# Attention and gated FFN on one core: four query/key buffers, one bias transfer for two heads, three value transfers issued first

## The chip, the cores and the metric

The kernel runs on one core of one Trainium2 chip. The metric is the device time of one execution in microseconds; the time before is the median of three executions.

## The reference

Four batches, eight heads, 576 positions, head size 64; then a gated FFN with 512 inputs and 1024 hidden columns. All inputs are float32.

```python
scores = scale * np.matmul(q, k.transpose(0, 1, 3, 2))
x = (psi_rel / psi_i)[..., None]          # log distances, from positions alone
h = np.maximum(x @ w1 + b1, 0.0)
bias = h @ w2                             # one value per (i, j, head)
scores = scores + bias.transpose(2, 0, 1)[None, :, :, :]
attn = softmax(scores)
y = np.matmul(attn, v)
# FFN on y: relu(y @ w_in), a 3-tap convolution along the sequence,
# h * sigmoid(conv), @ w_out
```

## The kernel before

**Bias first.** The bias depends on the positions and the head only. A first stage (some 66 us) computes it for all eight heads, 36 blocks of 16 rows, and writes it to a DRAM scratch tensor, bias_d (L292). Attention reads it back from there as tiles of 128 rows.

**Pairs and units.** Attention then goes over 16 pairs n = 0 to 15. A pair is two heads p (0 to 3) of one batch b, with b running fastest, so the heads change, and with them the bias tiles, between pairs 3 and 4, 7 and 8, 11 and 12. A pair has five units t = 0 to 4, of 128 rows each: unit 0 holds the 64 remaining rows of both heads, units 1 to 4 hold 128 rows of each head. The list of units is `flat`; the loop over it (L635 on) is written out by hand as a software pipeline. Step (n, t) issues the scores (L349, TensorE) and the `reduce` (L360, VectorE: scores plus bias, row minimum) of the unit two places on, the exponentials (L374, ScalarE) of the next unit, the transposes (L420) of its own unit, and some parts of the product with the values (L457). So the bias tile t of the next heads is first read at step (n, t − 2) of the last pair before them or of their own first pair; tile 4 is the last one that is read, at step (4, 2), (8, 2) or (12, 2).

**Order of issue.** Every engine works through its own instructions in order. Nearly all transfers are issued by SyncE (SP) on one queue, in the order in which the program lists them; an SP instruction that waits holds up all that stand behind it.

**What SP issues in a pair.** In step (n, 2): queries and keys of pair n + 2 (`load`, four transfers, L150 and L151, 950 KB), which go into the buffer of pair n, one of two in pool `q_p`, and so wait until TensorE has done the last scores of pair n, issued in the same step. In every second step a slice of the FFN's weights (`load_w`, L118, 256 KB), read by VectorE and ScalarE four to five steps later. In the steps where the loop issues the last reduce that reads a bias tile of the old heads: the same tile of the next heads (`load_bias`, tile 0 in L178, tiles 1 to 4 in L176, one transfer for each head, 128 rows of 2304 bytes). In (n, 2), last: the values of pair n + 1 (`load_v`, L165 to L168, four transfers, 288 KB), into the buffer of pair n − 1, after the last product that reads it (in the same step). In (n, 3) and (n, 4): the softmax sums of pair n − 1 out to DRAM (L483 to L485) and back, spread over the partitions (L490), for GpSimd (L497).

**Pool `raw_p`.** It has two buffers with the tag "raw". One is used as a staging tile in the bias stage, and both from pair 14 on for the FFN's split inputs (`x_parts`). Between these uses they stand empty.

Of the kernel before, what the change touches and what calls it, by code (L numbers as in the profile page):

```python
# [9 lines left out]
F32 = mybir.dt.float32  # L10
# [9 lines left out]
def attention_ffn_kernel(  # L20
# [11 lines left out]
    nc = tc.nc  # L32
    B, S, DM = out.shape
    NP = qk.shape[1]
    D = qk.shape[2]
# [3 lines left out]
    P = 128  # L39
    TL = S % P  # L40
# [6 lines left out]
    BW = S + 64  # L47
# [6 lines left out]
    KO = 2 * QW  # L54

    def halves(ap):
        return ap.rearrange("p (a b) -> p a b", a=2)

    def pool(stack, name, bufs, **kw):
        return stack.enter_context(tc.tile_pool(name=name, bufs=bufs, reuse_waits="tile", **kw))  # L60
# [7 lines left out]
    raw_p = pool(ctx, "raw", 2)  # L68
# [11 lines left out]
    bias_rows = bias_d[64:64 + S * (H * BW - 1)].rearrange("(i c) -> i c", c=H * BW - 1)  # L80
# [3 lines left out]
    NSEQ = len(seq)  # L84
# [49 lines left out]
    with tc.manual_schedule():  # L134
        att = ExitStack()
        q_p = pool(att, "q", 2)
# [4 lines left out]
        vts, qks, sms, biast = {}, {}, {}, {}  # L141


        def load(n):
            p, b = seq[n]
            qks[n] = t = q_p.tile([P, KO + S], F32, name="qk")
            keys = qk[b, p, :, KO:].rearrange("d (h a s) -> d a h s", h=2, a=2)
            for a in range(2):
                rows = slice(D * a, D * a + D)
                nc.sync.dma_start(t[rows, 0:KO], qk[b, p, :, 0:KO])  # L150
                nc.sync.dma_start(halves(t[rows, KO:]), keys[:, a])  # L151
# [10 lines left out]
        def load_v(n):  # L162
            p, b = seq[n]
            vts[n] = vt = v_t[n % 2]
            nc.sync.dma_start(vt[0:TL, 0:9], v[b, p, 0:TL, 0:9])  # L165
            nc.sync.dma_start(vt[TL:P, 0:4], v[b, p, TL:P, 0:4])
            nc.sync.dma_start(vt[TL:P, 5:9], v[b, p, TL:P, 5:9])
            nc.sync.dma_start(vt[TL:P, 9], v[b, p, TL:P, 4])  # L168

        def load_bias(p, t):  # L170
            bt = bias_p.tile([P, 2, S], F32, name="bt") if t else bias0_p.tile([P, 1, S], F32, name="bt0")
            for h in range(2):
                c = (2 * p + h) * BW
                if t:
                    i0 = TL + (t - 1) * P
                    nc.sync.dma_start(bt[:, h], bias_rows[i0:i0 + P, c:c + S])  # L176
                else:
                    nc.sync.dma_start(bt[TL * h:TL * h + TL, 0, :], bias_rows[0:TL, c:c + S])  # L178
            biast[p, t] = bt

# [151 lines left out]
        def scores(n, t, h):  # L332
            p, b = seq[n]
            qt = qks[n]
            if h == 0:
                if n not in sms:
                    sms[n] = sm_p.tile([P, 9], F32, name="sm")
                nms[n, t] = sm_p.tile([P, 2], F32, name="nm")
                new_sp(n, t)
            ps = psS.tile([P, 2, 512], F32, name="s")  # L340


            ops = [(h, h * QW + P * t, slice(0, P))] if t else [
                (hh, hh * (QW + TL), slice(TL * hh, TL * hh + TL)) for hh in range(2)
            ]
            for hh, qo, po in ops:
                for a in range(2):
                    rows = slice(D * a, D * a + D)
                    nc.tensor.matmul(  # L349
                        ps[po, a, 0:HS],  # L350
                        qt[rows, qo:qo + po.stop - po.start],
                        qt[rows, KO + hh * HS:KO + hh * HS + HS],
                        start=True,
                        stop=True,
                    )
            return ps

        def reduce(ps, n, t, h):
            bt = biast[seq[n][0], t]
            nc.vector.tensor_tensor_reduce(  # L360
                out=halves(spt[n, t][0][:, h]),
                in0=ps[:, :, 0:HS],
                in1=halves(bt[:, h]),
                op0=ALU.add,
                op1=ALU.min,
                scale=-scale,
                scalar=3.0e38,
                accum_out=nms[n, t][:, h:h + 1],
            )
# [34 lines left out]
        def side_transposes(side, n, t, sums):  # L404

            spf = spt[n, t][0]
            for a, ra in enumerate(halves_):
                tr = nc.tensor.transpose(side[:, a, HS:HS + TL].bitcast(F32R), spf[ra, 8 * P:9 * P], identr[ra, ra])  # L408
                after_exp(tr, n, t)
            if sums is not None:  # L410
                for a, ra in enumerate(halves_):
                    nc.tensor.transpose(side[:, a, HS + TL:HS + P], rr_t[sums % 2][ra], ident[ra, ra])
# [154 lines left out]
        def heads(t):  # L567
            return (0, 1) if t else (0,)
# [66 lines left out]
        for u, (n, t) in enumerate(flat):  # L635
            p, b = seq[n]
            ui = units.index(t)
            sums = n - 1 if ui == 2 and n else None
            side = None
            if u + 2 < NU:  # L640
                for h in heads(flat[u + 2][1]):
                    if side is not None:
                        reduce(side, *flat[u + 2], 0)
                    side = scores(*flat[u + 2], h)
            if t:
                if side is None:
                    side = psS.tile([P, 2, 512], F32, name="s")
                side_transposes(side, n, t, sums)
            if u + 2 < NU:
                reduce(side, *flat[u + 2], h)  # L650
            if u + 1 < NU:
                for h in heads(flat[u + 1][1]):
                    expo(*flat[u + 1], h)
                turned_sp(*flat[u + 1])
            transposes(n, t, side, sums)
            next(job_steps, None)

            parts = len(fill) if u < 5 else pv_share[ui]
            while fill and parts > 0:
                fill.popleft()()  # L660
                parts -= 1
            next(job_steps, None)
            del spt[n, t]
            if u + 2 >= NU:
                f = u + 2 - NU
                hs_ff[0, f] = ffn_in(0, f)
            if u == 1 or n and ui == 2 and n + 2 < NSEQ:
                load(2 if u == 1 else n + 2)
            if u in conv_weights:
                conv_weights[u]()  # L670

            for at, do in ((u - 7, "load"), (u - 11, "split")):
                job = at // 2
                if at % 2 == 0 or not 0 <= job < 4 * KC + 2 * FE:
                    continue
                if job < 4 * KC:
                    src, dst = w_in[job // 4 * P:job // 4 * P + P], wi[job // 4]
                else:
                    src, dst = w_out[(job - 4 * KC) // 2 * P:(job - 4 * KC) // 2 * P + P], wo[(job - 4 * KC) // 2]
                cs = slice(job % 4 * 256, job % 4 * 256 + 256) if job < 4 * KC else slice(job % 2 * 256, job % 2 * 256 + 256)  # L680
                if do == "load":
                    raw_w[job] = (e_p if job % 3 else woe_p).tile([P, 256, 2], I32, name="raw_w", tag="h")
                    load_w(raw_w[job], src[:, cs])
                else:
                    job_steps = split_w_steps(e_p, dst[:, :, cs], raw_w.pop(job), ("cv", "cv"))
            if u + 2 < NU:
                n2, t2 = flat[u + 2]
                p2, b2 = seq[n2]
                if b2 == B - 1 and p2 + 1 < NP:
                    load_bias(p2 + 1, t2)  # L690
            if ui == (0 if n > 1 else 1) and n > 0:
                invert(n - 1)
            if ui == (2 if n > 1 else 3) and 1 <= n and n + 1 < NSEQ:
                load_v(n + 1)
            if ui == 3 and n > 0:
                store_sums(n - 1)
            if ui == 4 and n > 0:
                spread_sums(n - 1)
            if ends_group(n, t):
                fill.extend(pv_parts(n, t > 2))  # L700

            if ui == 2 and n > 1:
                apply_norm(n - 2)
            if n == NSEQ - 2 and ui > 1:
                x_parts(0, ui - 2)
            if n == NSEQ - 1 and ui == 0:
                x_parts(0, 3)
            if n == NSEQ - 1 and ui in (1, 2):
                load_wo(FE - 1 + ui)
# [91 lines left out]
        for i, (b, f) in enumerate(steps):  # L801
            if b == 0 and f in (2, 4):
                c = FE - 1 + f // 2
# [10 lines left out]
            for c in range(KC):  # L814
# [5 lines left out]
                lambda f, gi, t=t: gs[b, f][:, gi, t * P:(t + 1) * P] for t in range(NT)  # L820
# [98 lines left out]
```

## Time and profile before

| | |
|---|---|
| median of three executions | 500.37 us (498.35 to 500.55) |
| the profiled execution | 503.5 us |
| its span, first to last instruction | 501.7 us |
| TensorE busy in the span | 481.3 us |
| granted TensorE clock, mean | 0.997 |
| attention, pair after pair | about 84 to 300 us |

The views give times in microseconds from the start of the span. PE is TensorE's matmuls, PEld its weight loads, DVE VectorE, ACT ScalarE, POOL GpSimd, SPq SyncE's queue of transfers. A row of a timeline gives start, length, engine, line, operation, what is written from what, and how often; in square brackets the engine's idle time before it and what ended that. A row of windows gives one stretch: its length, the busy time of each engine with its number of instructions, the granted clock (1.00 is 2.4 GHz, 0.50 is 1.2 GHz), the mean busy share of the 16 DMA engines, and what they moved in GB/s.

### The profile page before, as it was taken

What the parts mean: (1) busy time and instruction counts of PE and PEld (TensorE: products, weight loads), DVE (VectorE), ACT (ScalarE), POOL (GpSimd) and SP (SyncE); (2) the same over time, 40 slices, a digit from 0 to 9 for tenths busy, and PEclk for the clock granted to TensorE, in tenths of its full rate; (3) what the DMA queues carried; (4) which work ended last, traced back from release to release, by engine and by line L of the source; (5) the groups of instructions that cost most, each with busy time, mean ns of one, the idle gap of its engine ahead of it and who ended that gap; (6) DMA issues with size and microseconds to landing.
All of it is one profiled execution on the core that took longest, in us unless ns stands there. A gap on an engine that the chain in (4) does not pass through costs nothing.

```text
span 501.7 us, 11124 instructions
## 1 busy us (share of the span) xinstructions
PE 481.3 (96%) x4202; PEld 354.0 (71%) x4202; DVE 383.3 (76%) x875; ACT 311.8 (62%) x747; POOL 103.6 (21%) x121
## 2 busy tenths in 40 slices
PE   5988889999999999999899999899999999999997
PEld 3333346666666666666466679779998899899986
DVE  6999957788888988998588918993896189829920
ACT  5988777878888889888488738541541145215510
POOL 1000000103232323223235513650052003400000
PEclk9999999999999999999899999999999999999999
DMA  5689556488778977879672300002000200020011
GB/s 135 256 265 338 204 176 149 108 238 207 183 176 202 260 173 169 181 190 273 173 185 59 109 25 26 0 2 84 1 1 0 106 0 2 1 84 1 0 43 64
DMA packets 32793, 60.83 MB, mean 121 GB/s; under 512 B 5580, under 2 KB 12260, under 8 KB 32740
## 3 DMA queue, kind: packets, MB, share of 16 engines
q1 hardware_dynamic: 32356, 59.78, 42.6%
q8 instruction: 33, 0.54, 0.5%
q10 hardware_dynamic: 384, 0.35, 0.2%
q14 instruction: 20, 0.16, 0.1%
HBM read 44.12 MB, written 15.98 MB: 120 GB/s over the span
## 4 chain that ended last, share of the span: by engine, by line
PE 82%; DVE 6%; DMA 5%; ACT 4%; issue 2%; SPq 0%; DVEq 0%; ACTq 0%
PE s L518 17%; PE o L457 16%; PE tp L766 15%; PE s L349 14%; PE tp L420 8%; PE s L261 6%; PE o L766 4%; DMA bt<-bias_d 4%; ACT st L287 2%; DVE cv L741 2%; DVE sp L360 1%; DVE ptx L91 1%; PE s L408 1%; ACT y L240 1%; DMA pars<-in_par_dram 1%
## 5 line engine op out<-in xcount | busy, mean ns | idle before, releaser
L360 DVE CUSTOM_DVE_ANT_0 sp<-s,bt 128x576 f32<-128x576 f32 x144 | 104.2, 754 | 39.5 <-PE s L349 15.0
L374 ACT ACTIVATE sp<-sp,nm 128x576 f32<-128x576 f32 x144 | 110.0, 767 | 3.2 <-DVE nm L360 3.2
L518 PE MATMUL s<-xs,wi 128*128 128x288 f32 x768 | 103.8, 296 | 1.7 <-ACT h L530 1.7
L518 PEld LDWEIGHTS s<-xs,wi 128*128 128x128 f32 x768 | 102.8, 189 | 3.2 <-ACT h L530 1.9
L349 PE MATMUL s<-qk 64*128 64x288 f32 (+1 forms) x640 | 93.2, 431 | 4.4 <-DVE nm L360 3.6
L349 PEld LDWEIGHTS s<-qk 64*128 64x128 f32 (+1 forms) x640 | 46.9, 175 | 47.9 <-DVE nm L360 15.6
L766 PE MATMUL tp<-wo,g 128*128 128x512 f32 x288 | 70.5, 390 | 0.0
L420 PE MATMUL tp<-identr,sr 64*128 64x64 f32 x1184 | 64.4, 247 | 0.0
L741 DVE SCALAR_TENSOR_TENSOR cv<-h,cw,cv 128x575 f32<-128x575 f32 x64 | 60.5, 945 | 2.5 <-ACT cv L736 0.6
L766 PEld LDWEIGHTS tp<-wo,g 128*128 128x128 f32 x288 | 53.7, 188 | 11.6 <-DVE g L761 0.7
L420 PEld LDWEIGHTS tp<-identr,sr 64*128 64x128 f32 x1184 | 55.6, 136 | 5.7 <-issue 0.6
L457 PE MATMUL o<-ptx,vt 128*64 128x320 f32 x320 | 52.0, 454 | 1.2 <-ACT ptx L88 0.9
L497 POOL TENSOR_TENSOR x<-x,rb 128x576 f32<-128x576 f32 x16 | 23.5, 1469 | 135.4 <-DMA rb<-r_d 116.9
L261 PE MATMUL s<-y,pars 128*32 128x512 f32 (+8 forms) x352 | 46.7, 513 | 4.8 <-DVE y L244 2.1
L530 ACT ACTIVATE h<-s 128x576 f32<-128x576 f32 x32 | 20.8, 650 | 47.7 <-PE s L518 47.7
L244 DVE TENSOR_SCALAR y<-tl,inv,nb 128x512 f32<-128x512 f32 (+8 forms) x116 | 49.9, 508 | 0.1
L457 PE MATMUL o<-pty,vt 128*64 128x256 f32 x320 | 44.2, 393 | 0.0
L261 PEld LDWEIGHTS s<-y,pars 128*32 128x32 f32 x352 | 17.2, 115 | 32.1 <-DVE y L244 16.2
L747 ACT ACTIVATE cv<-cv 128x576 f32<-128x576 f32 x32 | 21.8, 683 | 28.4 <-DVE cv L741 28.4
L91 DVE COPY ptx<-tp 128x256 f32<-128x256 f32 (+1 forms) x64 | 32.0, 500 | 1.4 <-PE tp L420 1.2
L131 POOL TENSOR_SCALAR xs<-x 128x576 fp32r<-128x576 f32 x16 | 14.8, 926 | 81.5 <-PE s L518 81.5
L457 PEld LDWEIGHTS o<-ptx,vt 128*64 128x64 f32 x320 | 20.9, 139 | 15.0 <-issue 1.1
(75 smaller groups left out, 574.3 us busy)
## 6 DMA issues: line engine op xcount, KB each, us to landing
qk<-in_qk_dram SPq DMA_DIRECT2D x32, 320.0 KB
bt<-bias_d SPq DMA_DIRECT2D x32, 288.0 KB
bias_d<-st SPq DMA_DIRECT2D x14, 607.0 KB
qk<-in_qk_dram SPq DMA_DIRECT2D x32, 144.0 KB
rb<-r_d SPq DMA_DIRECT2D x32, 144.0 KB
raw_w<-in_moe_w_in_dram SPq DMA_DIRECT2D x16, 256.0 KB
out_dram<-o SPq DMA_DIRECT2D x16, 256.0 KB
raw_w<-in_moe_w_out_dram SPq DMA_DIRECT2D x12, 256.0 KB
```

The source lines that it names most:

```text
L91: nc.vector.tensor_copy(o, i)
L244: nc.vector.tensor_scalar(y, dist[:, 0:n], inv[:, ig:ig + 1], nb1, op0=ALU.mult, op1=ALU.max)
L261: nc.tensor.matmul(ps[32 * j:32 * j + 32, a // 512 if n > 512 else blk % 2, 0:min(n - a, 512)], w2b, ys[j][:, a:min(n, a + 512)], start=Tr ...
L349: nc.tensor.matmul(ps[po, a, 0:HS], qt[rows, qo:qo + po.stop - po.start], qt[rows, KO + hh * HS:KO + hh * HS + HS], start=True, stop=True,)
L360: nc.vector.tensor_tensor_reduce(out=halves(spt[n, t][0][:, h]), in0=ps[:, :, 0:HS], in1=halves(bt[:, h]), op0=ALU.add, op1=ALU.min, scale ...
L374: exps[n, t, h] = nc.scalar.activation(sp[:, h], sp[:, h], AF.Exp, bias=nm[:, h:h + 1], scale=-1.0, accum_out=sms[n][:, col:col + 1],)
L420: tr = nc.tensor.transpose(ps[a][:, TL * s:TL * s + TL].bitcast(F32R), spf[ra, j:j + P], identr[ra, ra])
L457: nc.tensor.matmul(po[D * h:D * h + D, 0:width], vt[:, slot, :], pt[:, blk, :], start=(c == 0), stop=(c == 4),)
L497: nc.gpsimd.tensor_mul(xb[b][:, p], xb[b][:, p], rbs.pop(n))
L518: nc.tensor.matmul(ps[:, a, 0:HS], wi[c][:, pw, cs], xss[b, c][:, px, a * HS:(a + 1) * HS], start=(i == 0), stop=(i == 3 * KC - 1),)
L741: nc.vector.scalar_tensor_tensor(out=cv[:, o:o + S - 1], in0=h[:, i:i + S - 1], scalar=cw[:, f, kk:kk + 1], in1=cv[:, o:o + S - 1], op0=AL ...
L766: nc.tensor.matmul(ps, lhs(f, gi), wo[f][:, wj, cs], start=(f == 0 and i == 0), stop=(f == FC - 1 and i == 2),)
```

## The change

Three things, all in what SP issues.

Queries and keys: pairs 2, 3, 6, 7, 10, 11 go to the two `raw_p` buffers, the others stay in `q_p`, so four pairs are held. Pairs 2, 3 and 4 are loaded in the loop's steps 1, 3 and 5, pair 5 in step (1, 2), and from there pair n + 4 in step (n, 2) as long as n + 4 is below 14. Steps (10, 2) and (11, 2) load nothing; pairs 14 and 15 are loaded in (12, 2) and (13, 2), as before.

Bias: tiles 1 to 4 come in one transfer for both heads (256 rows of 2304 bytes). Tile 0 keeps two transfers.

Values: three transfers instead of four (256 runs of 1024 bytes, then twice 64 runs of 256 bytes; the same 288 KB), issued as the first and no longer as the last of step (n, 2), so ahead of queries and keys, weights and bias.

```diff
@@ load(n)
-            qks[n] = t = q_p.tile([P, KO + S], F32, name="qk")
+            qk_pool, tag = (raw_p, "raw") if n % 4 > 1 and n < NSEQ - 4 else (q_p, "qk")
+            qks[n] = t = qk_pool.tile([P, KO + S], F32, name="qk", tag=tag)
@@ load_v(n)
-            nc.sync.dma_start(vt[0:TL, 0:9], v[b, p, 0:TL, 0:9])
-            nc.sync.dma_start(vt[TL:P, 0:4], v[b, p, TL:P, 0:4])
-            nc.sync.dma_start(vt[TL:P, 5:9], v[b, p, TL:P, 5:9])
+            by5 = [x.rearrange("p (g s) d -> p g (s d)", s=5)[:, :, 0:4 * D] for x in (vt, v[b, p, :, 0:10])]
+            nc.sync.dma_start(*by5)
+            nc.sync.dma_start(vt[0:TL, 4], v[b, p, 0:TL, 4])
             nc.sync.dma_start(vt[TL:P, 9], v[b, p, TL:P, 4])
@@ load_bias(p, t)
-            for h in range(2):
-                c = (2 * p + h) * BW
-                if t:
-                    i0 = TL + (t - 1) * P
-                    nc.sync.dma_start(bt[:, h], bias_rows[i0:i0 + P, c:c + S])
-                else:
+            k = 1 if p else 0
+            if t:
+                i0 = TL + (t - 1) * P
+                rows = bias_rows[i0:i0 + P, 2 * p * BW - k:2 * (p + 1) * BW - k]
+                nc.sync.dma_start(bt, rows.rearrange("i (h c) -> i h c", h=2)[:, :, k:k + S])
+            else:
+                for h in range(2):
+                    c = (2 * p + h) * BW
                     nc.sync.dma_start(bt[TL * h:TL * h + TL, 0, :], bias_rows[0:TL, c:c + S])
@@ the loop over the units
-            if u == 1 or n and ui == 2 and n + 2 < NSEQ:
-                load(2 if u == 1 else n + 2)
+            if ui == (2 if n > 1 else 3) and 1 <= n and n + 1 < NSEQ:
+                load_v(n + 1)
+            if u in (1, 3, 5):
+                load(u // 2 + 2)
+            if ui == 2 and 0 < n < NSEQ - 2:
+                if n + 4 < NSEQ - 2:
+                    load(n + 4)
+                elif n >= NSEQ - 4:
+                    load(n + 2)
...
-            if ui == (2 if n > 1 else 3) and 1 <= n and n + 1 < NSEQ:
-                load_v(n + 1)
```

## Rows read from the trace of the kernel before

**Rows 1.** The page, busy time of TensorE, share of the span, instructions.
```profile
PE 481.3 (96%) x4202; PEld 354.0 (71%) x4202; DVE 383.3 (76%) x875; ACT 311.8 (62%) x747; POOL 103.6 (21%) x121
```
**Rows 2.** Windows, pair by pair, each from step (n, 3) to the next one.
```profile
112.77:126.99 14.22, 14.22 (x166) 9.42 (x168) 12.20 (x37) 11.85 (x35) 4.76 (x7) 1.00 0.77 203
...
169.68:184.13 14.45, 14.23 (x164) 9.38 (x165) 12.91 (x36) 12.08 (x35) 4.60 (x7) 1.00 0.83 210
...
226.83:243.71 16.88, 14.47 (x166) 9.55 (x165) 11.70 (x36) 12.98 (x38) 4.62 (x7) 1.00 0.82 227
243.71:259.65 15.94, 15.94 (x166) 10.09 (x168) 12.68 (x38) 11.37 (x32) 3.96 (x6) 0.90 0.70 188
```
**Rows 3.** Timeline of VectorE and TensorE where pair 12's bias tile 4 is read.
```profile
241.13 0.76 DVE L360 CUSTOM_DVE_ANT_0 sp<-s,bt 128x576 f32<-128x576 f32 x1 [3.37 <-DMA bt<-bias_d]
...
241.96 0.81 PE L349 MATMUL s<-qk 64*64 64x288 f32 x8 [2.31 <-DVE nm L360]
...
243.71 3.45 PE L457 MATMUL o<-ptx,vt 128*64 128x320 f32 x12
...
259.58 1.84 PE L457 MATMUL o<-ptx,vt 128*64 128x320 f32 x12
```
**Rows 4.** Windows of 2 us around that wait.
```profile
236.00:238.00 2.00, 2.00 (x22) 1.28 (x20) 1.77 (x5) 1.97 (x7) 0.14 (x1) 1.00 1.07 278
...
240.00:242.00 2.00, 0.04 (x1) 0.04 (x1) 0.87 (x3) 0.48 (x3) 0.00 (x0) 1.00 0.12 36
...
244.00:246.00 2.00, 2.00 (x10) 0.92 (x9) 1.61 (x5) 1.36 (x4) 0.00 (x0) 0.50 0.81 199
```
**Rows 5.** Timeline of SP's queue, steps (10, 2) and (11, 2).
```profile
210.57 0.47 SPq L150 DMA_DIRECT2D qk<-in_qk_dram  x1
...
227.72 0.53 SPq L150 DMA_DIRECT2D qk<-in_qk_dram  x1
...
231.40 1.43 SPq L176 DMA_DIRECT2D bt<-bias_d  x2
```
**Rows 6.** Timeline of SP, VectorE and TensorE where the heads change after pair 7.
```profile
170.96 2.77 SPq L176 DMA_DIRECT2D bt<-bias_d  x2
...
178.78 0.47 SPq L168 DMA_DIRECT2D vt<-in_v_dram  x1
...
181.41 0.76 DVE L360 CUSTOM_DVE_ANT_0 sp<-s,bt 128x576 f32<-128x576 f32 x1 [0.87 <-DMA bt<-bias_d]
...
182.28 0.76 DVE L360 CUSTOM_DVE_ANT_0 sp<-s,bt 128x576 f32<-128x576 f32 x1
...
184.13 1.84 PE L457 MATMUL o<-ptx,vt 128*64 128x320 f32 x12 [0.23 <-ACT sp L374]
```
**Rows 7.** Windows of 2 us in the same stretch.
```profile
177.00:179.00 2.00, 2.00 (x30) 1.72 (x30) 1.89 (x8) 2.00 (x7) 0.00 (x0) 1.00 1.05 266
179.00:181.00 2.00, 2.00 (x20) 1.23 (x20) 1.54 (x5) 1.97 (x5) 0.37 (x1) 1.00 0.67 181
181.00:183.00 2.00, 2.00 (x36) 1.14 (x32) 1.49 (x5) 1.55 (x6) 0.77 (x2) 1.00 0.08 17
```
**Rows 8.** Timeline of VectorE where the heads change after pair 3.
```profile
123.74 0.76 DVE L360 CUSTOM_DVE_ANT_0 sp<-s,bt 128x576 f32<-128x576 f32 x1
...
124.42 0.75 DVE L360 CUSTOM_DVE_ANT_0 sp<-s,bt 128x576 f32<-128x576 f32 x1
```
**Rows 9.** Timeline of SP, VectorE and TensorE at the start of the loop.
```profile
68.75 1.64 SPq L176 DMA_DIRECT2D bt<-bias_d  x2
72.37 0.47 SPq L150 DMA_DIRECT2D qk<-in_qk_dram  x1
...
71.95 0.75 DVE L360 CUSTOM_DVE_ANT_0 sp<-s,bt 128x576 f32<-128x576 f32 x1
...
73.39 0.76 DVE L360 CUSTOM_DVE_ANT_0 sp<-s,bt 128x576 f32<-128x576 f32 x1 [0.68 <-DMA bt<-bias_d]
...
74.21 0.76 PE L349 MATMUL s<-qk 64*128 64x288 f32 x4 [0.69 <-DVE nm L360]
```

## The prediction, made before the changed kernel had run

> **What bounds the kernel now.** I read the page's busy times first. TensorE is busy 481.3 of 501.7 us [rows 1], so an edit that only moves transfers has 20.4 us of TensorE idle time to win from, plus whatever a low clock costs. The next view is the windows pair by pair. A pair takes 14.22 us with TensorE idle for nothing [rows 2], although VectorE, ScalarE and the DMA engines (share 0.77) are well used: attention is TensorE's, and a transfer matters only where it comes too late. Two places show it. From step (11, 3) on, two pairs take 16.88 + 15.94 = 32.82 us where two normal ones take 28.44 us: 4.4 us lost [rows 2]. After pair 7 a pair takes 14.45 us: 0.2 us lost.
>
> The timeline names the cause of the large loss. VectorE stands for 3.37 us before the reduce that first reads bias tile 4 of the last heads; TensorE, which needs the PSUM bank that this reduce frees, stands for 2.31 us, so about 1 us of VectorE's wait is covered [rows 3]. Then the same twelve value products take 3.45 us, a pair later 1.84 us [rows 3], and the windows show the granted clock at 0.50, the 1.2 GHz level, in 244 to 246 after this idle time [rows 4]. So 2.4 us are idle time and the rest of the 4.4 us is the clock's fall.
>
> Why is the tile late? SP issues it at 231.40 to 232.83, and it is read at 241.13: almost ten microseconds for 590 KB [rows 3, 5]. In the windows the DMA engines are full until shortly before that, 1.07 busy at 236 to 238, and nearly empty behind it, 0.12 [rows 4]. It is a backlog: the tile stands behind earlier bytes on the queue. Step (11, 2) issued 950 KB of queries and keys from 227.72 on, ahead of it, and step (10, 2) another 950 KB from 210.57 on [rows 5]. Neither is needed for a pair and more.
>
> **The change part by part.** *The two loads taken out of (10, 2) and (11, 2).* At about 200 GB/s (198 to 278 in these stretches, [rows 2, 4]) 950 KB are 4.7 us of queue time. The one at (11, 2) alone would bring the tile 4.7 us forward, against 3.37 us of lateness. The one at (10, 2) lets SP reach (11, 2) with an emptier queue. The other parts give some of that back (next paragraphs, 1.5 + 0.8 us), so 7 us or more against 3.37 us remain: the wait goes, with its clock fall. Gain 4.4 us; bounds 3.4 us (some of it remains) and 4.6 us. What is late next there: nothing, the pair is TensorE's again.
>
> *The same loads put elsewhere.* They start at the loop's steps 1 to 5, when pairs 2 to 5 come in. The first used is pair 2, as before; the others get three or more pairs of time. The DMA engines have room there, and what queues behind are sums for GpSimd. Nothing, unless the last bias tile of the first heads is touched (below). In steady state each pair still loads one pair: no byte is saved after pairs 3 and 7.
>
> *Which buffer.* Pair 5 is requested before pair 4. If the two buffers of `q_p` went round in turn, pair 8 would stand behind pair 5's last scores and hold up SP for five steps. I take it that a pool hands out the buffer whose last use lies behind in the program, which is pair 4's; the rival below prices the other reading.
>
> *Values first.* In (n, 2) SP now waits for the last value product of the step ahead of everything else, some 1.3 us later than the scores that it waited for before. Queued behind it are the new loads (four pairs early: harmless), the weight slice (four steps early) and, at a change of heads, bias tile 4. The last is the one with little slack. The values are (64·18)·256 B = 295 KB, and they now stand ahead of bias tile 4 instead of behind it. At 210 GB/s, the rate of the pair after pair 7 [rows 2], that is 1.4 us. The smaller runs (384 instead of 256 packets) add perhaps 0.1 to 0.2 us, so 1.5 us. The lower bound is 0: the windows show the queue run empty at 181 (share 0.67, then 0.08), with the values, issued up to 179.25, already moved by then, and bias tile 4's second half read at 182.28 [rows 6, 7]. If it is the emptying of the whole queue that lets the tile land, its place in the queue costs nothing. The first reading fits the backlog better, the second the landing times; I take 0.9 us, between them.
>
> The Trainium skill (DMA: Bandwidth & Descriptors, Queues, rings and completion order) says that on each DMA engine descriptors are consumed in ring order, and that a later one may still finish its write before an earlier one. By the first half the sum would take 1.5 us, by the second less; it speaks against putting the values first. The late tile behind its backlog agrees with the order [rows 3, 5].
>
> *One transfer for two heads.* It saves 16 issues of 0.4 to 0.8 us on SP, which is not the bound while the queue is full, so nothing. It costs something: the reduce of the first head used to start when its half had landed, and now waits for both. After pair 7 the halves were read at 181.41 (waited for) and 182.28 (0.9 us behind, where the first reduce takes 0.76) [rows 6]: 0.8 us. The same at the start, see below.
>
> The Trainium skill (DMA: Bandwidth & Descriptors, Bandwidth) asks for transfers of a megabyte and more, and shows 64 KB at 32 per cent and 1 MB at 78 per cent of the peak. By that the doubled tiles would move faster. The rows show engines already 1.05 busy with transfers of this kind [rows 7], and the runs of 2304 bytes stay as they are, so I take no gain.
>
> *Sum after pair 7.* VectorE waits 0.87 us now [rows 6]; 0.8 + 0.9 more is 2.6 us, bounds 1.7 and 3.2. The cover was 1.06 us in one place (3.37 against 2.31, [rows 3]) and 0.64 in the other (0.87 against 0.23, [rows 6]); with 0.85 TensorE stands for 1.7 us, bounds 0.8 and 2.4, where it stands 0.2 us now. That is +1.5 us if the clock holds. 2.31 us of standing were followed by a fall that cost the other 2.0 us of the 4.4, and 0.23 us were not [rows 2, 3, 4, 6]; 1.7 us lies nearer to the first, but I leave the fall to the range, which then has +0.6 and +4.2 us.
>
> *After pair 3.* The two reduces start at 123.74 and 124.42 back to back, with no wait [rows 8]: both halves had landed by then, how long before doesn't show. With 0.9 us of values ahead and both halves needed, VectorE waits 0 to 1.8 us, mostly covered: +0.3 us, bounds 0 and 1.0.
>
> *The start.* Tile 4 of the first heads is issued at 68.75. Its first half is read at 71.95 without a wait, its second at 73.39 after 0.68 us of waiting, and TensorE then stands for 0.69 us [rows 9]. In one transfer both land when the second half does, so the first reduce starts at about 73.3 and the second at 74.1 instead of 73.39: +0.7 us, on the path. Pair 2 now follows at once instead of at 72.37 [rows 9]; if it slows the tile, +2.0 us at most; if the tile, asked for in one go, lands earlier, 0.
>
> *Sum.* −4.4 + 1.5 + 0.3 + 0.7 = −1.9 us, made against the profiled 503.5 us: 501.6. The median of the runs is 3.1 us under that execution. I subtract the same 1.9 us from it: 500.4 − 1.9 = 498.5 us. Part of the 3.1 us may be this very wait, shorter without a profile; then the gain has less to take.
>
> **The rivals.** *Nothing given back.* The tile's landing is set by the emptying of the queue, the values cost nothing, and the clock holds: −4.4 + 0.6 + 0 + 0.4 = −3.4 us, 497.0 us. For it: the empty windows at 181 to 183 [rows 7]. Against it: the first half's lead is lost in any case.
>
> *The wait moves to pair 8 and takes the clock with it (slower).* The values and both halves stand in full, VectorE waits 3.2 us after pair 7, as it now does after pair 11, and TensorE's clock falls there: +4.2. After pair 3 +1.0, at the start +2.0, and of the gain 4.4 at most: +2.8 us, 503.2 us. It decides from the point where TensorE stands more than about 2 us. For it: 2.31 us were enough once [rows 3, 4].
>
> *The wait after pair 11 is small without a profile.* If the 3.1 us between the profiled and the usual execution are that wait, the gain is 1.3 us, the losses shrink alike, and the time stays at about 500 us.
>
> *The buffers go round in turn.* SP stands from step (4, 2) to (5, 2); the weight slice behind it lands at most some 2 us after VectorE wants it. That adds 0 to 2 us to the forecast: up to 500.5 us.
>
> **How the numbers follow.** The forecast has 0.43, nothing given back 0.33, the wait at pair 8 with the clock 0.10, the small wait 0.10, the buffers 0.04. A measurement of this kernel tells 0.5 per cent, 2.5 us, from no change. The forecast's own range is 497 to 500 us and lies below 497.9 in about a quarter of its cases; nothing given back nearly always does: 0.11 + 0.29 = 0.40 faster. Slower are most of the cases at pair 8: 0.08. The rest, 0.52, is the same. The range runs from 495.8 (nothing given back, and 1.2 us for the runs' own spread of 2.2 us) to 502.0 (just under the slower case).
>
> **What would show it.** In the changed profile: the windows at pairs 11 to 13 at 14.2 us with the clock at 1.00; no wait for a bias transfer before the reduce in step (12, 2); a longer one, 1.7 to 3.2 us, in step (8, 2), and a first one in (4, 2); in the window behind (8, 2) the clock at 1.00 or 0.50, which tells forecast from slower rival; the first reduce of tile 4 at the start waiting about 1.3 us. I am wrong if the wait after pair 11 stays, if the wait after pair 7 doesn't grow, or if SP shows a long wait in (4, 2).

## The result, and the profile after

The changed kernel is slower. Six executions have a median of 505.62 us (504.21 to 510.91), six of the kernel before 499.86 us; the ratio is 1.0134, 95 per cent interval 1.0108 to 1.0159. Ratios and intervals, here and below, compare mean times, so they can differ a little from the quotient of the medians beside them. The forecast was 498.5 us, the range ended at 502.0.

The profiled execution has a span of 505.2 us, 3.5 us over that of the kernel before in [rows 1] and 7.2 us over that of a second profile of it (498.0 us, further down). Windows pair by pair, cut as in [rows 2], show where it goes:

```profile
112.97:127.94 14.97, 14.36 (x166) 9.44 (x165) 11.64 (x36) 12.59 (x36) 4.81 (x7) 1.00 0.88 260
127.94:142.24 14.30, 14.30 (x166) 9.61 (x168) 12.95 (x38) 11.56 (x34) 3.98 (x6) 1.00 0.67 179
...
170.80:190.02 19.22, 15.23 (x166) 9.91 (x166) 13.61 (x39) 12.96 (x37) 5.46 (x8) 0.93 0.84 228
190.02:206.33 16.31, 16.31 (x167) 10.23 (x168) 11.86 (x35) 11.27 (x31) 3.06 (x6) 0.87 0.53 138
...
234.81:249.04 14.23, 14.23 (x166) 9.42 (x168) 13.54 (x37) 11.85 (x35) 5.96 (x8) 1.00 0.43 141
```

The pair from step (11, 3) on takes 14.23 us instead of 16.88: the loss there is gone. The two pairs from (7, 3) on take 19.22 + 16.31 = 35.53 us against 28.44 normal ones: 7.1 us lost, where it was 0.2. The two from (3, 3) on lose 14.97 + 14.30 − 28.44 = 0.8 us, where it was nothing. At the start TensorE stands 1.06 us instead of 0.69 [rows 9]. The sum is −4.4 + 6.9 + 0.8 + 0.4 = +3.7 us, against 3.5 measured.

```profile
73.80 1.43 PE L352 MATMUL s<-qk 64*128 64x288 f32 x8 [1.06 <-DVE nm L363]
```

The timeline of VectorE and TensorE where pair 8's bias tile 4 is first read, answering to [rows 3, 6]:

```profile
186.60 0.76 DVE L363 CUSTOM_DVE_ANT_0 sp<-s,bt 128x576 f32<-128x576 f32 x1 [5.05 <-DMA bt<-bias_d]
187.29 0.75 DVE L363 CUSTOM_DVE_ANT_0 sp<-s,bt 128x576 f32<-128x576 f32 x1
...
187.43 1.34 PE L352 MATMUL s<-qk 64*64 64x288 f32 x8 [3.99 <-DVE nm L363]
...
189.95 3.47 PE L460 MATMUL o<-ptx,vt 128*64 128x320 f32 x12
```

It is the picture of [rows 3], one change of heads earlier and larger: 5.05 us of waiting on VectorE, 3.99 us on TensorE, then value products at the slow clock. The forecast had 2.6 us of waiting.

SP's queue says why. This is its timeline from step (6, 2) to step (7, 2); the tile waited for is the last line:

```profile
152.53 0.39 SPq L167 DMA_DIRECT2D vt<-in_v_dram  x1
155.01 0.48 SPq L168 DMA_DIRECT2D vt<-in_v_dram  x1
155.54 0.59 SPq L169 DMA_DIRECT2D vt<-in_v_dram  x1
156.17 0.60 SPq L151 DMA_DIRECT2D qk<-in_qk_dram  x1
...
162.55 0.61 SPq L488 DMA_DIRECT2D r_d<-rt  x1
163.51 0.39 SPq L177 DMA_DIRECT2D bt<-bias_d  x1
166.55 1.13 SPq L493 DMA_DIRECT2D rb<-r_d  x2
...
168.40 0.90 SPq L177 DMA_DIRECT2D bt<-bias_d  x2
...
177.72 0.35 SPq L118 DMA_DIRECT2D raw_w<-in_moe_w_in_dram  x1
179.15 0.37 SPq L177 DMA_DIRECT2D bt<-bias_d  x1
```

SP issues the first piece of the values at 152.53 and then stands until 155.01: the second piece goes into the slot that the step's last value product reads. Queries and keys follow from 156.17; in the kernel before, the same step issued them from 152.68. That kernel's timeline of SP in the same steps:

```profile
152.68 0.47 SPq L150 DMA_DIRECT2D qk<-in_qk_dram  x1
...
163.20 1.12 SPq L490 DMA_DIRECT2D rb<-r_d  x2
...
165.01 1.85 SPq L176 DMA_DIRECT2D bt<-bias_d  x4
```

The windows of the changed kernel show the DMA engines run dry meanwhile, 0.07 busy at 155 to 157:

```profile
153.00:155.00 2.00, 2.00 (x34) 1.42 (x34) 1.89 (x8) 1.56 (x5) 1.72 (x3) 1.00 0.62 183
155.00:157.00 2.00, 2.00 (x31) 1.27 (x33) 1.97 (x7) 1.98 (x6) 0.78 (x1) 1.00 0.07 16
157.00:159.00 2.00, 2.00 (x16) 1.12 (x14) 0.88 (x3) 1.93 (x7) 0.97 (x2) 1.00 0.73 198
159.00:161.00 2.00, 2.00 (x30) 1.36 (x26) 2.00 (x6) 0.60 (x1) 0.16 (x1) 1.00 1.01 225
```

In the kernel before they are full in that window:

```profile
155.00:157.00 2.00, 2.00 (x24) 1.12 (x22) 2.00 (x5) 1.97 (x7) 0.51 (x1) 1.00 1.04 242
```

The delay then grows. The sums go out behind the late queries and keys, and SP, before it may read them back, stands until 166.55 (163.20 before). Bias tiles 2 and 3 follow at 168.40 (165.01 before), the values, queries, keys and weights of (7, 2) behind them, and tile 4 at 179.15 instead of 170.96 [rows 6]. Of these 8.2 us, 3.4 are there at tiles 2 and 3. The rest comes in step (7, 2), where the values take SP from 169.34 to 172.33 and SP then stands 1.9 us before the weights and 1.1 us before tile 4. For its reader the tile is 5 us late. The waits of SP show both waits in total over the execution (engine, line, waited for: us, times, longest):

```profile
SPq L493 <- DMA r_d<-rt: 36.8, 20, 3.7
...
SPq L168 <- PE o L460: 18.1, 9, 2.1
SPq L167 <- PE o L460: 12.8, 9, 4.0
```

In the kernel before, the wait for the sums was 10.5 us in 14 times, the longest 1.0.

### The profile page after: what moved, and what is told of

It is laid out like the page before. It is cut to its first block, busy times and chain, and to the rows that moved or that the text cites. A ratio compares the mean times of both kernels' runs of the same rounds, so it can differ in the third digit from the quotient of the medians.

```text
span 505.2 us, 11040 instructions
## 1 busy us (share of the span) xinstructions
PE 482.3 (95%) x4202; PEld 354.0 (70%) x4202; DVE 385.5 (76%) x875; ACT 311.5 (62%) x747; POOL 103.6 (21%) x121
## 4 chain that ended last, share of the span: by engine, by line
PE 72%; DMA 6%; DVE 5%; issue 1%; ACT 1%; DVEq 0%; SPq 0%; ACTq 0%
PE s L521 17%; PE tp L774 15%; PE o L460 15%; PE s L352 12%; PE tp L423 7%; PE o L774 4%; DMA vt<-in_v_dram 3%; DMA bt<-bias_d 3%; DVE sp L363 1%; DVE cv L749 1%; PE s L411 1%; DVE cv L756 1%; DVE ptx L91 1%; DVE g L769 0%; DVE w L103 0%
## 5 line engine op out<-in xcount | busy, mean ns | idle before, releaser
L88 ACT ACTIVATE pty<-tp 128x512 f32<-128x512 f32 x32 | 18.8, 589 | 21.7 <-PE tp L423 21.7
```

## The experiments

Three theories were put against each other. HOLD: with the values first, SP stands at them until the step's last value product, and everything behind it comes later. QUEUE: the values' bytes stand ahead of the bias on the queue, wait or no wait. SHAPE: the merged bias transfer and the smaller runs of the values. Each time stands beside the kernel before, measured on the same chip in the same series. In the edits `...` stands for lines left out; those of the runs called "and nothing else" start from the kernel before, the others from the changed kernel.

### Values back in their old place

```diff
-            if ui == (2 if n > 1 else 3) and 1 <= n and n + 1 < NSEQ:
-                load_v(n + 1)
             if u in (1, 3, 5):
...
+            if ui == (2 if n > 1 else 3) and 1 <= n and n + 1 < NSEQ:
+                load_v(n + 1)
             if ui == 3 and n > 0:
```

> The changed kernel with the values moved back to their old place, behind weights and bias; everything else as changed. Three theories of why the changed kernel loses 4 us of TensorE time after pair 7. HOLD: SP waits at the values for the step's last value product, so queries, keys, sums and bias are all issued later, the DMA engines run empty meanwhile, and the last bias tile comes late. QUEUE: it is the values' bytes and transfers standing ahead of the bias, wait or no wait. SHAPE: it is the merged bias transfer and the smaller runs of the values. HOLD and QUEUE: VectorE's wait for bias in step (8, 2) falls from 5.05 us to 0.9 to 1.7 us, no wait after pair 11, 495 to 498 us. SHAPE: the wait stays above 3 us, 503 to 506 us.

Measured: 499.45 us against 499.67, ratio 1.0011 (0.9989 to 1.0032). VectorE waits 0.40 us in step (8, 2):

```profile
181.71 0.76 DVE L363 CUSTOM_DVE_ANT_0 sp<-s,bt 128x576 f32<-128x576 f32 x1 [0.40 <-DMA bt<-bias_d]
```

So the order of issue is the loss, and SHAPE falls as its cause. But the time is not the expected 495 to 498 us: with the loss gone, nothing is won either. That became the second question.

### Values first and nothing else

```diff
+            if ui == (2 if n > 1 else 3) and 1 <= n and n + 1 < NSEQ:
+                load_v(n + 1)
             if u == 1 or n and ui == 2 and n + 2 < NSEQ:
                 load(2 if u == 1 else n + 2)
...
-            if ui == (2 if n > 1 else 3) and 1 <= n and n + 1 < NSEQ:
-                load_v(n + 1)
```

> The kernel before, with nothing changed but the values' place: first in step (n, 2). HOLD and QUEUE: bias tile 4 comes late after pairs 3, 7 and 11, each with 2 to 5 us of wait on VectorE, 504 to 512 us. SHAPE: at most 1 us over the kernel before, 499 to 501 us.

Measured: 507.54 us against 499.67, ratio 1.0150 (1.0120 to 1.0180). The place of one group of transfers, in the kernel before, costs more than the whole change did. After pair 7 VectorE waits 2.74 us and TensorE 1.69; after pair 11 TensorE stands 0.90 us; after pair 3, 0.29 us at the scores. The time is in the expected range; a wait of 2 to 5 us at each of the three places is not, only the one after pair 7 is of that size:

```profile
184.41 0.76 DVE L360 CUSTOM_DVE_ANT_0 sp<-s,bt 128x576 f32<-128x576 f32 x1 [2.74 <-DMA bt<-bias_d]
...
185.23 1.31 PE L349 MATMUL s<-qk 64*64 64x288 f32 x8 [1.69 <-DVE nm L360]
```

### Three value buffers

```diff
-        v_t = [vz_p.tile([P, 2 * NT + 2, D], F32, name=f"vt{i}") for i in range(2)]
+        v_t = [vz_p.tile([P, 2 * NT + 2, D], F32, name=f"vt{i}") for i in range(3)]
...
-            vts[n] = vt = v_t[n % 2]
+            vts[n] = vt = v_t[n % 3]
```

> The changed kernel with three value buffers instead of two: the values are still issued first, but the buffer that they go into was last read a pair earlier, so SP does not wait for a product there. HOLD: wait in step (8, 2) down to 0.9 to 2 us, 496 to 499 us. QUEUE and SHAPE: as the changed kernel, 4 to 5 us of wait, 504 to 507 us.

Measured: 499.03 us against 499.67, ratio 0.9998 (0.9977 to 1.0018). This separates HOLD from QUEUE: the values are still first, with the same bytes ahead of the bias, and only the wait is gone. SP's timeline in the same steps:

```profile
150.90 0.42 SPq L167 DMA_DIRECT2D vt<-in_v_dram  x1
151.38 0.48 SPq L168 DMA_DIRECT2D vt<-in_v_dram  x1
...
152.74 0.47 SPq L151 DMA_DIRECT2D qk<-in_qk_dram  x1
...
173.89 0.37 SPq L177 DMA_DIRECT2D bt<-bias_d  x1
```

The window in which the engines had run dry:

```profile
155.00:157.00 2.00, 2.00 (x26) 1.17 (x22) 1.90 (x5) 1.97 (x7) 0.01 (x1) 1.00 1.05 244
```

Queries and keys go out at 152.74, as in the kernel before; the engines are 1.05 busy at 155 to 157 instead of 0.07; tile 4 is issued at 173.89 instead of 179.15, and VectorE does not wait for it. SP's second wait, the one for the sums, is still there in full:

```profile
SPq L493 <- DMA r_d<-rt: 36.7, 17, 3.7
```

So that wait comes with the new order and not only with late loads, and by itself it costs nothing here.

### Queries and keys ahead of the values

```diff
-            if ui == (2 if n > 1 else 3) and 1 <= n and n + 1 < NSEQ:
-                load_v(n + 1)
             if u in (1, 3, 5):
                 load(u // 2 + 2)
...
                     load(n + 2)
+            if ui == (2 if n > 1 else 3) and 1 <= n and n + 1 < NSEQ:
+                load_v(n + 1)
```

> The changed kernel with the values behind queries and keys but still ahead of weights and bias. HOLD: queries and keys go out as soon as the scores are done, as in the kernel before, so little of the shift is left: wait in step (8, 2) 1 to 2.5 us, 497 to 500 us. QUEUE: the bias has as much ahead of it as in the changed kernel, 4 to 5 us of wait, 503 to 507 us. SHAPE: the same as QUEUE.

Measured: 499.70 us against 499.67, ratio 1.0023 (0.9987 to 1.0060), and no wait for bias after pairs 3, 7 and 11 in the profiled execution. The values still stand ahead of weights and bias, and still wait; but 950 KB are on the queue while SP stands. HOLD expected such a time, with 1 to 2.5 us of waiting left in step (8, 2); QUEUE did not. Three of its ten executions took 503.7 to 507.4 us, so at times something still comes late; none of these three has a trace.

### Only the small pieces first

```diff
-            by5 = [x.rearrange("p (g s) d -> p g (s d)", s=5)[:, :, 0:4 * D] for x in (vt, v[b, p, :, 0:10])]
-            nc.sync.dma_start(*by5)
             nc.sync.dma_start(vt[0:TL, 4], v[b, p, 0:TL, 4])
             nc.sync.dma_start(vt[TL:P, 9], v[b, p, TL:P, 4])
...
+        def load_v_main(n):
...
+            if ui == (2 if n > 1 else 3) and 1 <= n and n + 1 < NSEQ:
+                load_v_main(n + 1)
             if ui == 3 and n > 0:
```

> The changed kernel with only the two 16 KB pieces of the values first in the step and the 256 KB piece in the old place, behind weights and bias. The small ones carry the wait for the step's last value product, with a ninth of the bytes. HOLD: nearly as slow as the changed kernel, 503 to 506 us, and 3 to 5 us of wait in step (8, 2). QUEUE: the bytes no longer stand ahead of the bias, 498 to 500 us.

Measured: 506.86 us against 499.57, ratio 1.0144 (1.0103 to 1.0184). Two transfers of 16 KB at the head of the step, with the bulk of the values behind the bias, cost as much as the whole change. So it is the wait that costs, and not the bytes. VectorE waits 2.47 us after pair 3 and 3.90 us after pair 7:

```profile
188.16 0.76 DVE L367 CUSTOM_DVE_ANT_0 sp<-s,bt 128x576 f32<-128x576 f32 x1 [3.90 <-DMA bt<-bias_d]
```

### The sums read back two steps later

```diff
-            if ui == 4 and n > 0:
+            if ui == 1 and n > 1:
+                spread_sums(n - 2)
+            if ui == 4 and n == NSEQ - 1:
                 spread_sums(n - 1)
```

> The changed kernel with the reading back of the softmax sums put two steps later, into step (n + 1, 1); nothing else. In the changed kernel SP stands there up to 3.7 us, because the sums' way out stands behind late queries and keys. CHAIN: this second wait of SP is what carries the delay on to the bias; without it the wait in step (8, 2) falls from 5.05 us to 0.5 to 2.5 us, 498 to 501 us. FIRST WAIT ALONE: the wait at the values delays the bias by itself, 3.5 to 5 us of wait remain, 503 to 506 us.

Measured: 500.36 us against 499.57, ratio 1.0013 (0.9989 to 1.0037). The first wait is all there, 17.7 and 11.4 us in total at lines 168 and 167; but SP no longer stands at the sums ahead of the bias:

```profile
157.09 0.60 SPq L151 DMA_DIRECT2D qk<-in_qk_dram  x1
...
165.81 1.96 SPq L177 DMA_DIRECT2D bt<-bias_d  x2
...
176.65 0.37 SPq L177 DMA_DIRECT2D bt<-bias_d  x1
...
183.08 0.76 DVE L363 CUSTOM_DVE_ANT_0 sp<-s,bt 128x576 f32<-128x576 f32 x1 [0.38 <-DMA bt<-bias_d]
```

Queries and keys are as late as in the changed kernel or later (157.09), tiles 2 and 3 are issued at 165.81 instead of 168.40, tile 4 at 176.65 instead of 179.15, and the wait of 5.05 us is 0.38. The loss after pair 7 takes both waits of SP, one after the other; either of them taken away gives nearly all of it back. The smaller one after pair 3 stays in this run: VectorE waits 1.52 us there, 1.51 in the changed kernel.

### The kernel before, once more

No edit.

> The kernel before, profiled a second time. Its spans over many executions are 496.6 to 499.3 us, while the execution that the prediction rests on had 501.7 us. OUTLIER: the 4.4 us lost after pair 11 are not what a usual execution loses; here VectorE waits there 0 to 1.5 us, span 497 to 499 us. USUAL: the wait is 3 us or more again and the span is over 500 us.

Measured: 499.83 us, span 498.0 us. Its timeline of SP and VectorE at the change of heads after pair 11:

```profile
227.74 0.85 SPq L176 DMA_DIRECT2D bt<-bias_d  x2
...
237.39 0.76 DVE L360 CUSTOM_DVE_ANT_0 sp<-s,bt 128x576 f32<-128x576 f32 x1
```

The windows of the two pairs around it:

```profile
226.34:240.58 14.24, 14.24 (x167) 9.43 (x165) 13.47 (x37) 11.85 (x34) 4.68 (x7) 1.00 0.86 222
240.58:254.82 14.24, 14.24 (x168) 9.44 (x166) 13.29 (x37) 12.18 (x36) 3.94 (x6) 1.00 0.74 186
```

The reduce that waited 3.37 us in [rows 3] doesn't wait; tile 4 is issued 3.7 us earlier than in [rows 5]; the two pairs take 28.48 us instead of 32.82. The 4.4 us on which the forecast rested were in that execution, not in a usual one: of the 23 executions measured beside this one, two took more than 503 us. Why the tile was issued late in that execution stays open.

### The four buffers and nothing else

```diff
-            qks[n] = t = q_p.tile([P, KO + S], F32, name="qk")
+            qk_pool, tag = (raw_p, "raw") if n % 4 > 1 and n < NSEQ - 4 else (q_p, "qk")
+            qks[n] = t = qk_pool.tile([P, KO + S], F32, name="qk", tag=tag)
...
-            if u == 1 or n and ui == 2 and n + 2 < NSEQ:
-                load(2 if u == 1 else n + 2)
+            if u in (1, 3, 5):
+                load(u // 2 + 2)
+            if ui == 2 and 0 < n < NSEQ - 2:
+                if n + 4 < NSEQ - 2:
+                    load(n + 4)
+                elif n >= NSEQ - 4:
+                    load(n + 2)
```

> The kernel before, with nothing changed but the four buffers of queries and keys and the time of their loads. My prediction gave this part a gain of 4.4 us. If only executions with a late bias tile after pair 11 have that to lose, and few do: 498.6 to 499.5 us, 0.2 to 1 us under the kernel before, with no wait for bias after pair 11. If the gain is real: 495 to 496.5 us.

Measured: 501.24 us against 499.64, ratio 1.0033 (1.0011 to 1.0055). Both expectations missed: the part that was to bring the gain costs 0.3 per cent. In the profiled execution (span 498.7 us) no bias tile is late after pairs 3, 7 and 11. At the start TensorE stands 0.18 + 0.85 us, more than in [rows 9], with the bias tiles not merged:

```profile
73.10 0.76 PE L350 MATMUL s<-qk 64*128 64x288 f32 x4 [0.18 <-DVE nm L361]
74.71 0.76 PE L350 MATMUL s<-qk 64*128 64x288 f32 x4 [0.85 <-DVE nm L361]
```

What makes its usual execution longer was not found; its twelve executions spread from 498.99 to 503.95 us.

### The merged bias transfer and nothing else

```diff
-            for h in range(2):
-                c = (2 * p + h) * BW
-                if t:
-                    i0 = TL + (t - 1) * P
-                    nc.sync.dma_start(bt[:, h], bias_rows[i0:i0 + P, c:c + S])
...
+            if t:
+                i0 = TL + (t - 1) * P
+                rows = bias_rows[i0:i0 + P, 2 * p * BW - k:2 * (p + 1) * BW - k]
+                nc.sync.dma_start(bt, rows.rearrange("i (h c) -> i h c", h=2)[:, :, k:k + S])
```

> The kernel before, with nothing changed but the bias: one transfer for both heads. My prediction priced this at +0.7 us at the start and some 0.6 us after pair 7. PRICE RIGHT: 500.2 to 501.2 us, a wait of about 1.3 us at the start and of 1 to 2 us in step (8, 2). FREE: 499 to 500 us, waits as in the kernel before.

Measured: 501.59 us against 499.64, ratio 1.0055 (1.0024 to 1.0086). The merged transfer costs 1.95 us by the medians, 2.7 us by the ratio. In the profiled execution, a short one of 500.36 us, VectorE waits after pair 3 and after pair 7:

```profile
125.52 0.76 DVE L362 CUSTOM_DVE_ANT_0 sp<-s,bt 128x576 f32<-128x576 f32 x1 [1.72 <-DMA bt<-bias_d]
...
182.80 0.76 DVE L362 CUSTOM_DVE_ANT_0 sp<-s,bt 128x576 f32<-128x576 f32 x1 [1.13 <-DMA bt<-bias_d]
```

The second wait was expected, the first was not. TensorE stands 0.97 us at the start, 0.68 us after pair 3 and not at all after pair 7. Half of the twelve executions took 502.4 to 507.1 us, and none of them has a trace; what they lose is not shown.

### Bias first in the step

The best order that the runs pointed to: three value buffers, weights and bias ahead of values, queries and keys, one bias transfer for each head. The edit of the loop:

```diff
+            if ui == (2 if n > 1 else 3) and 1 <= n and n + 1 < NSEQ:
+                load_v(n + 1)
+            if u in (1, 3, 5):
+                load(u // 2 + 2)
...
             if ui == 3 and n > 0:
                 store_sums(n - 1)
```

> The changed kernel with three value buffers, weights and bias first in the step, then values, then queries and keys, and the bias again in one transfer for each head. All theories: no wait for bias after pairs 3, 7 and 11, and the start as before. Then the time is that of an execution in which nothing comes late, 498.3 to 499.0 us, against 499.7 us of the kernel before, whose executions lose 0 to 2.5 us. If its runs spread over more than 2 us, something else than bias tile 4 comes late now and then.

Measured: 499.39 us against 499.57, ratio 0.9985 (0.9964 to 1.0006). No bias tile is late after pairs 3, 7 and 11; at the start VectorE waits 1.12 us, not less than before [rows 9]. Its twelve executions lie within 498.64 and 500.45 us, those of the kernel before in the same series within 498.85 and 504.47. Its longest execution is shorter; on the whole its time can't be told from that of the kernel before. No version was found that beats the kernel before.

## Why the prediction was wrong, point by point

**What bounds the kernel.** The chain was read rightly: TensorE, and a bias tile that lands late. What failed is the step from one execution to the usual one. The prediction had noted 3.1 us between the profiled 503.5 us and the median, and that part of it might be this very wait, and still subtracted the whole. The second execution shows no wait there. The rival "the wait is small without a profile" read the gain rightly, and it had a chance of 0.10; its time, about 500 us, was wrong, because it let the losses shrink too.

**Taking out the two loads.** Gain priced at 4.4 us. In the profiled pair of executions it came, 16.88 to 14.23 us, but that is luck: the first of the two executions happened to have the loss. Against the usual execution there was next to nothing to gain, and the buffers alone cost 1.0033.

**Values first.** This is the term that was mis-sized. The prediction saw SP's wait, some 1.3 us later than the scores, and listed what stands behind it, but gave the wait no price (18.1 us in 9 times in the changed profile): only the bytes and runs of the values were priced, 0.9 us on the tile's landing (0 to 1.5). The wait was also looked at only in the step that issues tile 4, (7, 2). One pair earlier, in (6, 2), the engines run dry, and queries and keys start 3.5 us later (152.68 to 156.17). What this term measures by itself is 507.54 − 499.67 = 7.9 us in the kernel before. Then the second queue was not followed: the sums' way out stands behind those loads, and SP stands for it once more. The prediction named what is queued behind the values, but stopped at the end of that step and left this wait for the sums out. The bytes cost nothing that shows: with three buffers they stand ahead of the bias and no wait follows. Hence the sentence on the order of descriptors was weighed at the wrong place; it is SP's own order that did it.

**After pair 7.** Priced +1.5 us (+0.6 to +4.2), measured 7.1 − 0.2 = +6.9 us, the clock's fall included, beyond that range. The slower rival had the place and the mechanism's end (pair 8, the clock), with the wrong start (bytes and merged halves), a price too small and a chance of 0.10. Its point for the clock, more than about 2 us of standing, was too high as well: the level fell after 1.69 us in one run (last section).

**After pair 3.** Priced +0.3 us (0 to 1.0), measured +0.8 us. **The start.** Priced +0.7 us (0 to 2.0), measured 1.06 − 0.69 = +0.4 us. Both lie in their ranges, but the causes priced are not shown. After pair 3 the price was for the values' bytes and the merged halves; with three value buffers both are still there and no tile is late. At the start it was for the merged halves; the four buffers alone, without the merge, stand 1.03 us there.

**One transfer for two heads.** Priced by the lost lead of the first half, some 1.3 us in all at the start and after pair 7; alone it costs 501.59 − 499.64 = 1.95 us. The sign is right and the size a little small; the places are not shown, since the executions that make the median longer have no trace.

**The buffers' order.** Pair 8 does not stand behind pair 5: its queries and keys go out at 128.44, right behind the values of step (4, 2); SP has no wait for the values' product longer than 4.0 us, and the cost of the change vanishes with the value buffers alone.

## What to carry to other kernels

A transfer that must wait for a buffer belongs behind everything that could go at once, or gets one buffer more: on an in-order queue the wait costs what stands behind it, not what it moves. Look for it in every step, not only in the one with the late transfer: here it starved the engines a pair earlier. Follow a delayed queue through every later wait on the same queue, here the reading back of sums that went out behind the late loads. And before a loss in a profile becomes a gain in a forecast, compare the profiled time with the median: a difference nearly as large as the loss (here 3.1 and 4.4 us) says that the loss may be that execution's own.

## What the runs showed of the hardware that was not expected

TensorE's clock did not fall by the length of the idle time alone. With the values first and nothing else, 1.69 us of standing at 185 were followed by the lower level, 1.2 GHz; with the values back in their old place, 1.77 us at 74 were followed by none. At the same place of the loop, 1.61 us were followed by the lower level in the run with the sums read back later. In these two TensorE had been equally busy just before (1.82 us of 68 to 70, all of 70 to 72), so the rows don't show what decides. The row of the first is shown under "Values first and nothing else"; a window behind it:

```profile
187.00:189.00 2.00, 2.00 (x20) 1.34 (x20) 1.89 (x6) 1.24 (x4) 0.07 (x1) 0.50 0.64 181
```

The standing with the values in their old place, and the windows behind it:

```profile
74.32 1.43 PE L352 MATMUL s<-qk 64*128 64x288 f32 x8 [1.77 <-DVE nm L363]
...
74.00:76.00 2.00, 1.68 (x20) 1.15 (x20) 1.96 (x7) 1.66 (x5) 0.00 (x0) 1.00 1.09 234
76.00:78.00 2.00, 1.78 (x24) 1.21 (x20) 1.97 (x8) 1.70 (x5) 0.00 (x0) 1.00 1.03 219
```

The same with the sums read back two steps later:

```profile
74.28 1.70 PE L352 MATMUL s<-qk 64*128 64x288 f32 x8 [1.61 <-DVE nm L363]
...
76.00:78.00 2.00, 2.00 (x24) 1.73 (x22) 1.97 (x8) 1.08 (x3) 0.00 (x0) 0.50 1.03 222
```
